# Folding both heads' softmax sums before the summing matmul, in the first four of eight batches

## The chip, the core and the metric

The kernel runs on one core of one Trainium2 chip. The metric is the time of one execution on the device in microseconds (us); lower is better. The core's engines are TensorE (PE, matmuls and transposes), VectorE (DVE), ScalarE (ACT), GpSimd (POOL) and SyncE (SP, which here only issues DMAs). Each engine takes its instructions in program order and waits on semaphores for the others.

## The reference

Blockwise causal attention, whose output feeds a mixture-of-experts layer with one expert for each token.

```python
# attention: batch 8, heads 8, sequence 576, head size 64, block 64
scores = scale * np.matmul(q, k.transpose(0, 1, 3, 2))
scores = np.where(mask, scores, -1e9)          # key block <= query block
attn = np.exp(scores - max); attn /= attn.sum(-1) + 1e-09
out = np.matmul(attn, v)                       # -> x: (8, 576, 512)

# experts: 8 of them, 512 -> 1024 -> 512
logits = x @ w_gate                            # (8, 576, 8)
local_gate = sigmoid(x @ w_local)
for b in range(B):
    for s in range(S):
        e = argmax(logits[b, s]) if s == 0 or local_gate[b, s] < 0.5 else prev_e
        out[b, s] = softmax(logits[b, s])[e] * (relu(x[b, s] @ w1[e]) @ w2[e])
```

## The kernel before, in words

**Attention.** The 64 heads are taken as 32 pairs, four pairs to a batch; the main loop runs over the pairs, `i = 0 .. 31`, with `b, r = divmod(i, 4)`. Order within each engine is the order of the program text. A pair's 576 keys are cut in five chunks (four of 128, one of 64) that lie on the partitions; the 576 queries lie along the free axis. So the exponentials of the scores stand as (keys, head, queries). Those of chunk 0 are written to `Ss[i]`, a 128 x 2 x 576 float32 tile from a ring of three (`Sall`), those of chunks 1 to 4 to `Pc[i % 2]`.

**One iteration** does, in this order: `load_qk(i + 2)` (SP's DMA queue); `values(i - 1)` (TensorE, L920, then a ScalarE copy to `oT`); `add_chunks(i - 1)` (VectorE, L932: four adds put chunks 1 to 4 onto `Ss[i - 1]`, in place, so they wait until `values` has read chunk 0); `load_v(i + 1)` (SP); `scores` and `exps` of pair `i` (TensorE L882, ScalarE L892, with GpSimd clearing the masked corners, L869, in `clear`); `transposes(i + 1)` of queries and keys (TensorE L844, ScalarE L839, and the VectorE copy L850 of the last 64 tokens); a task of the routing, if there is one; and `arrange(i + 2)`, two GpSimd copies (L810) that reorder the loaded queries and keys, followed in some iterations by a load of expert weights (L107, L111) on GpSimd's DMA queue. `load_qk` writes a staging buffer that `arrange` must have read first, so its DMA waits on SP for GpSimd, and what stands behind it on SP waits too. In iteration 1 alone `values(i - 1)` comes after the scores and `add_chunks(i - 1)` after the transposes (`swap`).

**The sums.** After `add_chunks`, row k of `Ss[i][:, h]` holds, for each query, the exponentials of the keys k, k + 128, ... of head h. The softmax's denominator is the sum of these over the 128 partitions. `half_batch(b, a)` (L696) takes it on TensorE together with the gate logits of two pairs, in one PSUM bank of four 32-row strips (two pairs, two ranges of 320 queries). It has three terms of four matmuls each: one that multiplies `oT` with the gate weights `wg2`, and two, one for each head, that multiply `Ss[i][:, h]` with a shifted view of `sel`, a tile that has a column of ones; the shift decides whether the sum lands in the head's row E + 1 or 16 + E + 1 of the strip. VectorE then copies the bank out (L704). The first half of a batch (pairs 0 and 1) is done at `r == 2`, the second half at `r == 0` of the next batch; each needs the sums of pair `i - 1`, whose adds run in the same iteration. At `r == 1` and `r == 3` the tasks are the logits' transposes and the rows of x (L718, L710, L757).

**Routing and experts.** From `slot >= 17.5` on VectorE also does the routing tables (`tokens`, `slots_first`), with scratch space in the last expert's part of `w1_bf`, which is loaded late for that reason. After pair 31 the expert stage runs over tiles of 128 gathered tokens (L994, L1128, gathers L653 and scatters L1135 on GpSimd).

Of the kernel before, what the change touches and what calls it, by code (L numbers as in the profile page):

```python
# [62 lines left out]
def kernel(  # L63
# [11 lines left out]
    nc = tc.nc  # L75
    F32 = mybir.dt.float32
# [5 lines left out]
    B, H, S, D = q.shape  # L82
# [4 lines left out]
    E = moe_w_gate.shape[1]  # L87
    F = moe_w1.shape[2]
    BS = B * S
    P = 128  # L90
# [11 lines left out]
    w1_bf = w_p.tile([P, E * KO1 * F], BF16, tag="w1", name="w1_bf")  # L102
    w2_bf = w_p.tile([P, E * FO * Dm], BF16, tag="w2", name="w2_bf")
    WE = KO1 * F
# [10 lines left out]
    HP = H // 2  # L115
# [31 lines left out]
    rt_c = ctx.enter_context(tc.tile_pool(name="rt_const", bufs=1))  # L147
# [3 lines left out]


    sel = rt_c.tile([P, 48], F32, tag="sel", name="sel")
    more_g = rt_c.tile([P, 256], F32, tag="more_g", name="more_g")

    wg2 = rt_c.tile([P, HP, 32], F32, tag="wg2", name="wg2")
# [519 lines left out]
    def bank(nm):  # L676
        return banks["of"](nm)
# [7 lines left out]
    def half_batch(b, a, gates=True, sums=True):  # L685


        ps = bank("trg")
        terms = [lambda i: (wg2[:, i % HP, :], oTs[i])] * gates + [
            lambda i, h=h: (sel[:, 16 - 16 * h:48 - 16 * h], Ss[i][:, h]) for h in range(2)] * sums  # L690
        for j, term in enumerate(terms):
            for p in range(2):
                w, x = term(HP * b + 2 * a + p)
                for g, q0 in enumerate((0, QA)):
                    o = 64 * g + 32 * p
                    nc.tensor.matmul(ps[o:o + 32, :QB], lhsT=w, rhs=x[:, q0:q0 + QB],  # L696
                                     start=(j == 0), stop=(j == len(terms) - 1))

        def out():
            if not gates:  # L700
                nc.vector.tensor_add(LT[b, a], LT[b, a], ps[:, :QB])
                return
            LT[b, a] = op.tile([P, QB], F32, tag="LT%d" % a, name="LT%d" % a, bufs=1)
            (nc.vector.tensor_copy if sums else nc.scalar.copy)(LT[b, a], ps[:, :QB])  # L704
        return out
# [41 lines left out]
    def rows_out(b, t):  # L747
        n = CW[t]
        ps = bank("trx")
        for p in range(HP):  # L750
            turn(ps, P * p, oTs[HP * b + p], t)

        def out():

            x = (xgs[t][:, :XH] if b < NB1 + 1 or (b < B - 1 and t == NX - 1)
                 else op.tile([P, XH], F32, tag="x", name="x"))
            nc.vector.tensor_mul(x[:n].bitcast(BF16).rearrange("p (h d) -> p h d", d=D),  # L757
                                 ps[:n].rearrange("p (h d) -> p h d", d=D),
                                 rcp(b, t)[:, :, None].to_broadcast([n, H, D]))
            r0 = b * S + P * t  # L760
            store(x_dram[r0:r0 + n, :XH], x[:n])
        return out

    oTs, rs, LT, Ss = ({} for _ in range(4))

    with tc.tile_pool(name="atn_const", bufs=1) as cst, \
# [13 lines left out]
        def constants():  # L780
            nc.vector.memset(sel, 0.0)
            nc.vector.memset(sel[:, 16 + E + 1:16 + E + 2], 1.0)
            nc.vector.memset(L[64:, :, :], 0.0)

        raws, vs = ({} for _ in range(2))
# [27 lines left out]
        def load_v(i):  # L813
            if i >= NPAIR:
                return
            b, p = divmod(i, HP)
            m = ld.tile([P, 4, 2, D], F32, tag="v4", name="v4", bufs=NV)
            for h in range(2):
                nc.sync.dma_start(
                    out=m[:, :, h, :],  # L820
                    in_=v[b, 2 * p + h, :512].rearrange("(so si) d -> si so d", si=P))
            nc.sync.dma_start(out=vls[i % NV][:ST],
                              in_=v[b, 2 * p:2 * p + 2, 512:].rearrange("h s d -> s h d"))
            vs[i] = [m, vls[i % NV]]
# [101 lines left out]
        def add_chunks(i):  # L926
            if not 0 <= i < NPAIR:
                return
            for c in range(1, NC):
                n = S - P * c  # L930
                rows = slice(0, CW[c])
                nc.vector.tensor_add(Ss[i][rows, :, P * c:], Ss[i][rows, :, P * c:],  # L932
                                     Pc[i % 2][rows, :, POS[c]:POS[c] + n])

        def tasks(i):

            b, r = divmod(i, HP)
            if r == 0 and b:
                return [[lambda: half_batch(b - 1, 1)]]
            if r == 1 and b:  # L940
                return [[lambda: logits(b - 1, 0), lambda: logits(b - 1, 1)],
                        [lambda t=t: rows_out(b - 1, t) for t in (0, 1)]]
            if r == 2:
                return [[lambda: half_batch(b, 0)]]
            if r == 3 and b:
                return [[lambda t=t: rows_out(b - 1, t) for t in (2, 3)],
                        [lambda: rows_out(b - 1, 4)]]
            return []
# [24 lines left out]
        sums = [Sb[(NPAIR + j) % NSB].rearrange("p h s -> p (h s)") for j in (1, 2, 0)]  # L973
# [28 lines left out]
        def expert(ph, j, engines=(mybir.EngineType.PE, mybir.EngineType.DVE)):  # L1002
            return nc.values_load(
                et_i[ph][0:1, j:j + 1], engines=engines, min_val=0,
                max_val=(E - 1) * WE,
                skip_runtime_bounds_check_because="the table is clamped to the last expert")

        def bf(x, n):
            return x.rearrange("p a s -> p (a s)").bitcast(BF16)[:, :n]
# [27 lines left out]
        def behind(i):  # L1037

            values(i - 1)
            if not swap:  # L1040
                add_chunks(i - 1)
            load_v(i + 1)
            steps.vector(1.4)

        for i in range(NPAIR):
            slot[0] = i
            load_qk(i + 2)


            swap = i == 1  # L1050
            if not swap:
                behind(i)
            if i == NPAIR - 1:

                tiles = [(0, j) for j in range(NS[0])] + [(1, j) for j in range(NS[1])]
                ev = {j: expert(*tiles[j]) for j in range(2)}
                w = weights_at(bf(Pc[0], WE), ev[0])

                free = bf(Sb[(NPAIR - 3) % NSB], 2 * S * 2)[:, -AHEAD * Dm:]
                xTs = {}  # L1060
                for j in range(AHEAD):
                    xTs[j] = free[:, j * Dm:(j + 1) * Dm].rearrange("p (k n) -> p k n", k=KO1)
                    nc.sync.dma_start(out=xTs[j], in_=row_of_x(xgs[j]), transpose=True)
            for u in range(len(UNITS)):
                exps(i, u, scores(i, u))
                if u == 0:
                    last_scores(i)
                    if i == 0:
                        transposes(1, nc.vector.tensor_copy)
                        constants()  # L1070
                        for h in range(2):
                            hs = slice(64 * h, 64 * h + 64)
                            nc.sync.dma_start(
                                out=wg2[hs, :, 16 * h:16 * h + E],
                                in_=moe_w_gate.rearrange("(p h d) e -> h d p e", h=2, d=D)[h])
                            nc.sync.dma_start(
                                out=wg2[hs, :, 16 * h + E:16 * h + E + 1],
                                in_=moe_w_local.rearrange("(p h d) e -> h d p e", h=2, d=D)[h])
            if swap:
                behind(i)  # L1080
            if i:
                transposes(i + 1, nc.scalar.copy)
            if swap:
                add_chunks(i - 1)
            for x in pending.pop(0) if pending else []:
                x()
            steps.tensor()
            steps.vector(2.0)
            for group in tasks(i):
                half.clear()  # L1090
                for out in [x() for x in group]:
                    out()
            slot[0] = i + 0.5
            if i == NPAIR - 1:

                w_next = weights_at(qkT.rearrange("p j a s -> p (j a s)").bitcast(BF16)[:, :WE],
                                    ev[1])
            steps.tensor()
            steps.vector(2.7)
            arrange(i + 2, [nc.gpsimd.tensor_copy] * 2)  # L1100

            if i == 1 + 25 * wload // 13 and wload < 2 * E - 2:
                load_weights(*divmod(wload, 2))
                wload += 1
            if i == NPAIR - 2:

                load_weights(E - 1, 1)
# [13 lines left out]
    with tc.tile_pool(name="ffn_s", bufs=2) as f_p, \  # L1121
# [148 lines left out]
        i = len(tiles) - 1  # L1270
# [31 lines left out]
```

## Time and profile before

| | us |
|---|---|
| three runs | 445.13, 449.56, 449.73 (median 449.56) |
| the profiled execution | 444.11 |
| its span, first to last instruction | 442.2 |
| TensorE busy (matmuls) | 423.8 (96% of the span) |
| VectorE busy | 255.1 (58%) |
| ScalarE busy | 257.6 (58%) |
| GpSimd busy | 185.3 (42%) |
| add_chunks, L932, 128 adds on VectorE | 90.3 |
| summing term, L696, 256 records trg<-S | 21.3 |
| arrange, L810, 61 copies on GpSimd | 44.2 |

A row of the profile names the line, the engine, the operation, the tile written and the tiles read, the shape and a count; `x` ahead of a number is that count. "idle before" is how long the engine stood still before the row's instructions, with what ended most of it behind an arrow. A busy TensorE is not one at its peak, since its matmuls overlap. The names `w1_bf` and `w2_bf` both appear as `w_bf`, and the staging buffer of queries and keys lies in `w2_bf`, so `w_bf<-in_k_dram` is a load of keys and `w_bf<-w_bf` a copy of `arrange`.

### The profile page before, as it was taken

Reading aid. Unit: us, or ns where it says so; the run is one execution under the profiler, and the core shown is the slowest. Engines: PE = TensorE matmul, PEld = TensorE weight load, DVE = VectorE, ACT = ScalarE, POOL = GpSimd, SP = SyncE. Lnnn points to the kernel's source line nnn. Section 1 sums busy time; section 2 is a strip of 40 time slices with the busy share of each in tenths; the row PEclk is TensorE's granted clock in tenths of the full one; section 3 lists DMA queues with packets and bytes.
Section 4 is the critical chain, followed back from the end, with each engine's and each line's share of the span. In section 5 each row is a group of like instructions: output and inputs, shape, how many; then the busy total and the mean of one; then the engine's idle time right before and its main releaser. Section 6 shows DMA issues by size and latency. Waiting matters only on the chain.

```text
span 442.2 us, 11716 instructions
## 1 busy us (share of the span) xinstructions
PE 423.8 (96%) x4260; PEld 309.3 (70%) x4281; DVE 255.1 (58%) x554; ACT 257.6 (58%) x409; POOL 185.3 (42%) x309
## 2 busy tenths in 40 slices
PE   8997999999999999999999999999799999999995
PEld 6775777677687676776776778657577767767763
DVE  3362454563563467868789976887788433333320
ACT  3763676577567656665677567534354545555552
POOL 2433423223212312123323514315757777767733
PEclk9997999999999999999999999999999999999999
DMA  5598399889799897986989884972847465556441
GB/s 161 138 209 167 92 199 190 187 185 181 182 180 185 181 190 174 191 125 145 183 171 215 156 217 75 188 130 87 167 133 159 114 159 137 147 142 151 134 104 72
DMA packets 113817, 69.65 MB, mean 157 GB/s; under 512 B 77024, under 2 KB 106208, under 8 KB 113761
## 3 DMA queue, kind: packets, MB, share of 16 engines
q1 hardware_dynamic: 96352, 37.94, 37.8%
q0 software_dynamic: 17408, 30.96, 34.9%
q8 instruction: 36, 0.59, 0.6%
q14 instruction: 21, 0.16, 0.1%
HBM read 66.88 MB, written 14.70 MB: 184 GB/s over the span
## 4 chain that ended last, share of the span: by engine, by line
PE 64%; DMA 14%; POOL 8%; issue 7%; ACT 4%; DVE 2%; POOLq 1%; SPq 1%; ACTq 0%; DVEq 0%
PE o L920 19%; PE sc L882 17%; PE trg L696 6%; PE kq L844 6%; DMA xg<-x_rows,idx 6%; PE ps_h L994 5%; POOL xg L653 5%; PE ps_y L1128 4%; DMA v<-in_v_dram 3%; PE trx L710 3%; POOL out_dram L1135 2%; DMA xT<-xg 2%; ACT Pc L892 2%; DMA w_bf<-in_q_dram 1%; DMA w_bf<-in_k_dram 1%
## 5 line engine op out<-in xcount | busy, mean ns | idle before, releaser
L932 DVE TENSOR_TENSOR S<-S,Pc 128x896 f32<-128x896 f32 (+3 forms) x128 | 90.3, 706 | 21.0 <-PE o L920 12.8
L882 PE MATMUL sc<-qkT 64*128 64x288 f32 (+3 forms) x768 | 98.8, 390 | 0.1
L882 PEld LDWEIGHTS sc<-qkT 64*128 64x128 f32 x768 | 68.8, 187 | 14.0 <-ACT qkT L839 0.5
L979 DVE COPY w1c<-w_bf 128x4096 bf16 x36 | 44.5, 1236 | 57.3 <-PE ps_h L994 53.7
L994 PEld LDWEIGHTS <-w1c 128*128 128x128 bf16 x1152 | 67.0, 98 | 13.0 <-issue 4.1
L994 PE MATMUL ps_h<-xT,w1c 128*128 128x128 bf16 x1088 | 66.3, 219 | 4.2 <-DMA xT<-xg 2.9
L924 ACT COPY oT<-o 128x576 f32<-128x576 f32 x32 | 20.5, 639 | 84.8 <-PE o L920 73.9
L1128 PE MATMUL ps_y<-w_bf,hT 128*128 x283 | 67.6, 379 | 1.1
L653 POOL DMA_INDIRECT xg<-x_rows,idx x38 | 56.1, 1477 | 23.1 <-issue 10.2
L839 ACT COPY qkT<-kq 128x1024 f32<-128x1024 f32 (+1 forms) x31 | 64.7, 2087 | 1.8 <-PE kq L844 1.6
L892 ACT ACTIVATE Pc<-sc 128x448 f32<-128x448 f32 (+1 forms) x96 | 63.9, 707 | 0.0
L810 POOL COPY w_bf<-w_bf 128x512 f32<-128x512 f32 x61 | 44.2, 745 | 44.1 <-DMA w_bf<-in_k_dram 20.0
L997 ACT ACTIVATE hT<-ps_h 128x512 bf16<-128x512 f32 x76 | 45.3, 597 | 29.4 <-PE ps_h L994 26.1
L920 PE MATMUL o<-Pc,v 128*64 128x320 f32 (+2 forms) x512 | 59.8, 373 | 0.0
L1135 POOL DMA_INDIRECT out_dram<-y,idx x38 | 44.1, 1160 | 35.3 <-ACT y L1133 20.2
L920 PEld LDWEIGHTS o<-Pc,v 128*64 128x64 f32 x512 | 36.9, 140 | 23.5 <-issue 0.2
L1133 ACT ACTIVATE y<-ps_y,xg 128x512 f32<-128x512 f32 x38 | 26.1, 688 | 45.1 <-PE ps_y L1128 43.2
L892 ACT ACTIVATE S<-sc 128x576 f32<-128x576 f32 x64 | 41.6, 650 | 15.6 <-PE sc L882 15.6
L1128 PEld LDWEIGHTS <-hT 128*128 128x128 bf16 x304 | 28.2, 98 | 27.7 <-issue 0.5
L869 POOL MEMSET Pc<- 64x128 f32 x96 | 17.5, 200 | 63.4 <-ACT Pc L892 59.4
L920 PE MATMUL o<-S,v 128*64 128x256 f32 (+1 forms) x256 | 39.7, 425 | 3.4 <-DMA v<-in_v_dram 2.5
L869 POOL MEMSET S<- 64x128 f32 x32 | 6.4, 200 | 86.5 <-ACT S L892 85.3
(287 smaller groups left out, 424.8 us busy)
## 6 DMA issues: line engine op xcount, KB each, us to landing
w_bf<-in_moe_w_dram POOLq DMA_DIRECT2D x16, 1024.0 KB, 10.4
w_bf<-in_k_dram SPq DMA_DIRECT2D x32, 256.0 KB, 3.6
w_bf<-in_q_dram SPq DMA_DIRECT2D x32, 256.0 KB, 4.5
v<-in_v_dram SPq DMA_DIRECT2D x64, 128.0 KB, 3.0
x_rows<-xg SPq DMA_DIRECT2D x24, 128.0 KB, 5.1
qkl<-in_k_dram SPq DMA_DIRECT2D x32, 32.0 KB, 3.7
qkl<-in_q_dram SPq DMA_DIRECT2D x32, 32.0 KB, 7.7
vl<-in_v_dram SPq DMA_DIRECT2D x32, 32.0 KB, 2.7
```

Source lines behind the costliest of these rows:

```text
L653: nc.gpsimd.indirect_dma_start(out=x, out_offset=None, in_=x_dram[:rows], in_offset=bass.IndirectOffsetOnAxis(ap=row_of(ph, j), axis=0), b ...
L810: copies[j](m, raws[i][1 + j].rearrange("p h j d -> p j h d"))
L839: copy(qkTs[i % 2][:, parts, :512].rearrange("p a (s j) -> p a j s", j=4), ps.rearrange("p a (j s) -> p a j s", j=4))
L882: nc.tensor.matmul(ps[:, h, col:col + n], lhsT=t[r, 0, c * P:c * P + P], rhs=t[r, 1, q0:q0 + n], start=True, stop=True)
L892: nc.scalar.activation(exps_at(i, c, q0, n, rows), ps[rows, :, col:col + n], func=AF.Exp, scale=scale_attn)
L920: nc.tensor.matmul(po[64 * h:64 * h + 64, VO + q0:VO + q0 + n], lhsT=vv, rhs=exps_at(i, c, q0, n, slice(0, P))[:, h, :], start=(c == 0), s ...
L932: nc.vector.tensor_add(Ss[i][rows, :, P * c:], Ss[i][rows, :, P * c:], Pc[i % 2][rows, :, POS[c]:POS[c] + n])
L979: nc.vector.tensor_copy(w, w1_bf[:, bass.ds(ev, WE)])
L994: nc.tensor.matmul(ps[:, fo, :], lhsT=w[:, ko * F + f0:ko * F + f0 + P], rhs=xT[:, ko, :], start=(ko == 0), stop=(ko == KO1 - 1))
L997: nc.scalar.activation(hT[:, half * (FO // 2):(half + 1) * (FO // 2), :], ps, func=AF.Relu)
L1128: nc.tensor.matmul(ps, lhsT=hT[:, fo, :], rhs=w2_bf[:, bass.ds(ev + fo * Dm, Dm)], start=(fo == 0), stop=(fo == FO - 1))
L1135: st = nc.gpsimd.indirect_dma_start(out=out_flat, out_offset=bass.IndirectOffsetOnAxis(ap=row_of(ph, j), axis=0), in_=y, in_offset=None, b ...
```

## The change

For pairs 0 to 15 the partitions' halves exchange their sums. `exchange(i)` has GpSimd copy the upper 64 partitions of head 0's sums to the lower 64 partitions of a buffer `swapped`, and the lower 64 of head 1's to the upper 64. `fold(i)` has VectorE add them, in place: afterwards the lower 64 partitions of `Ss[i][:, 0]` hold head 0's sums over 64 rows, and the upper 64 hold head 1's. One matmul term with `sel2`, a tile with a one in row E + 1 for the lower partitions and in row 16 + E + 1 for the upper, then gives both heads' denominators. `exchange` stands right behind `add_chunks` in the program, ahead of the iteration's clears and of `arrange` on GpSimd; `fold` stands behind the scores and ahead of the transposes, so ahead of L850 on VectorE (in iteration 1 both follow `add_chunks`). `swapped`, two buffers of 128 x 576 float32, lies at the end of the last expert's part of `w1_bf`. Batches 4 to 7 stay as they were.

```diff
+    sel2 = rt_c.tile([P, 32], F32, tag="sel2", name="sel2")
+
+    FOLDED = 4 * (H // 2)
...
         ps = bank("trg")
-        terms = [lambda i: (wg2[:, i % HP, :], oTs[i])] * gates + [
-            lambda i, h=h: (sel[:, 16 - 16 * h:48 - 16 * h], Ss[i][:, h]) for h in range(2)] * sums
+        terms = [lambda i: (wg2[:, i % HP, :], oTs[i])] * gates
+        if sums and HP * b < FOLDED:
+            terms += [lambda i: (sel2, Ss[i][:, 0])]
+        elif sums:
+            terms += [lambda i, h=h: (sel[:, 16 - 16 * h:48 - 16 * h], Ss[i][:, h])
+                      for h in range(2)]
...
             nc.vector.memset(sel[:, 16 + E + 1:16 + E + 2], 1.0)
+            nc.vector.memset(sel2, 0.0)
+            for h in range(2):
+                nc.vector.memset(sel2[64 * h:64 * h + 64, 16 * h + E + 1:16 * h + E + 2], 1.0)
...
+        swapped = w1_bf[:, E * WE - 4 * S:].bitcast(F32).rearrange("p (u s) -> p u s", u=2)
+
+        def exchange(i):
+            if 0 <= i < FOLDED:
+                for h in range(2):
+                    nc.gpsimd.tensor_copy(swapped[64 * h:64 * h + 64, i % 2],
+                                          Ss[i][64 - 64 * h:128 - 64 * h, h])
+
+        def fold(i):
+
+            if 0 <= i < FOLDED:
+                for h in range(2):
+                    r = slice(64 * h, 64 * h + 64)
+                    nc.vector.tensor_add(Ss[i][r, 0], Ss[i][r, h], swapped[r, i % 2])
...
             if not swap:
                 add_chunks(i - 1)
+                exchange(i - 1)
             load_v(i + 1)
...
             if swap:
                 behind(i)
+            else:
+                fold(i - 1)
             if i:
                 transposes(i + 1, nc.scalar.copy)
             if swap:
                 add_chunks(i - 1)
+                exchange(i - 1)
+                fold(i - 1)
```

## The prediction

> **What bounds the kernel now.** I read the page's busy table first, then the chain that ended last, then one stretch of time in the attention stage, then the groups of instructions kept apart by shape. The page says that TensorE is nearly always occupied and that most of the chain runs through it:
>
> ```profile
> PE 423.8 (96%) x4260; PEld 309.3 (70%) x4281; DVE 255.1 (58%) x554; ACT 257.6 (58%) x409; POOL 185.3 (42%) x309
> ...
> PE 64%; DMA 14%; POOL 8%; issue 7%; ACT 4%; DVE 2%; POOLq 1%; SPq 1%; ACTq 0%; DVEq 0%
> ```
>
> The chain between 120 and 140 us holds TensorE alone, so a microsecond taken from TensorE there is a microsecond of the kernel, and a microsecond that TensorE waits is one lost. Two pieces of it:
>
> ```profile
> 134.73 1.75 PE trg L696 x24
> 136.49 2.85 PE o L920 x28
> ```
>
> The first is one half_batch. In the timeline its gate term and its two sum terms stand apart, beside what GpSimd and VectorE do:
>
> ```profile
> 130.32 2.99 DVE L932 TENSOR_TENSOR S<-S,Pc 128x896 f32<-128x896 f32 x4
> ...
> 134.66 0.75 PE L696 MATMUL trg<-oT,wg 128*32 128x320 f32 x8
> 134.92 0.35 POOL L869 MEMSET Pc<- 64x128 f32 x2 [1.82 <-ACT Pc L892]
> 135.23 1.26 PE L696 MATMUL trg<-S,sel 128*32 128x320 f32 x16
> 135.34 1.18 POOL L810 COPY w_bf<-w_bf 128x512 f32<-128x512 f32 x2
> 136.41 0.20 PEld L920 LDWEIGHTS o<-S,v 128*64 128x64 f32 x4 [0.52 <-POOL w_bf L810]
> ```
>
> The gate term starts at 134.66, the sum terms at 135.23, the next work at 136.41. Two sum terms take 1.18 us, one takes 0.59. (A matmul shows as two records; 432 ns each is a latency, they overlap.) The adds of add_chunks end at 133.31, some 2.2 us before the first matmul that reads the newer pair's sums.
>
> **What is removed.** In eight half-batches (two for each of batches 0 to 3) four of twelve matmuls go: 8 x 0.59 = 4.7 us of TensorE. This is the ceiling of the gain, 1.05% of 449.6.
>
> **What is added, for each of 16 pairs.** Two GpSimd copies and two VectorE adds, each 64 x 576. The adds: the 896 form alone takes 1.09 us and the 384 form 0.56, so 1.04 ns for an element and 0.76 us for 576; two in a row overlap by 0.08, as the pair of L757 does (1.27 for 2 x 0.68), so 1.44. The copies: the nearest row is L810, 512 elements, 1.17 or 1.18 us for two; by length 1.31 for two of 576. No row shows a copy that moves data to other partitions. Its lower bound is that 1.31. For an upper bound I take twice that, 2.6, as near the 2.59 us that two L810 copies took when VectorE was in their way. I use 1.31, the same engine, type and kind, and keep 2.6 for the range. Three memsets of sel2 lie in iteration 0, where VectorE is idle for 6.39 us before L850: nothing, and 0.3 us if that cover were gone.
>
> **Copies and adds take turns.** One stretch shows what these two engines do to each other:
>
> ```profile
> 51.53 2.03 POOL L810 COPY w_bf<-w_bf 128x512 f32<-128x512 f32 x2
> 51.78 2.46 DVE L932 TENSOR_TENSOR S<-S,Pc 128x896 f32<-128x896 f32 x2 [0.71 <-PE o L920]
> ```
>
> The first copy took 0.61, the second 1.48: it ended only after the first add had. The two adds took 1.31 and 1.04 in place of 1.09 and 0.83. So a copy that is under way holds back an add, a copy that waits gets in between two adds, and each such copy costs VectorE some 0.22. In the new chain the second copy starts before the first fold add is released, so the order is copy, copy, add, add. With E the end of the adds: copies end at E + 1.31, the first fold add at about E + 1.95 (part of its fixed time is spent waiting), the second at E + 2.65. TensorE needs it for the second pair's matmul, the third of its sum term, 0.29 after the sum term starts.
>
> **Who is behind.** On VectorE the tail copy L850 stands behind the folds and ends up to 1.2 us later; its reader is scores of the next iteration, over 3 us on: hidden. On GpSimd the clears (L869), arrange (L810) and the weight DMA issue stand behind exchange; the clears had ended 1.5 us before values needs them at 136.41, and GpSimd was idle 4 to 5 us ahead of them, so in the steady part arrange starts where it did. On SP load_qk waits for arrange, load_v stands behind load_qk; this matters only at the start.
>
> **The sum, in three kinds of half-batch.** (1) Second halves, i = 4, 8, 12, 16: the adds end early (i = 8: 80.49; folds 83.14; needed 83.89; at i = 16 149.54, 152.19, 152.58), so the full 0.59 is gained: -2.4. (2) First halves, i = 6, 10, 14: VectorE is busy with the logits and rows of the batch before, adds end at 64.59, 99.22, 133.31; folds at 67.24, 102.09, 136.18 (in the last two an arrange copy comes in between, +0.22); needed at 66.82, 101.17, 135.52. With 0.1 for the signal TensorE waits 0.5, 1.0 and 0.8, 2.3 in all, against 3 x 0.59 = 1.8 saved: +0.5. Bounds: no wait, -1.8; each arrange copy ahead of a fold by its full 0.59, +1.6. (3) The first half-batch, i = 2, where two pairs' sums follow each other without a gap:
>
> ```profile
> 19.28 6.34 DVE L932 TENSOR_TENSOR S<-S,Pc 128x896 f32<-128x896 f32 x8
> ...
> 19.40 2.59 POOL L810 COPY w_bf<-w_bf 128x512 f32<-128x512 f32 x2 [2.69 <-DMA w_bf<-in_k_dram]
> 21.94 0.96 POOL L107 DMA_DIRECT2D w_bf<-in_moe_w_dram  x1
> ```
>
> Now: adds(0) end at 22.3, exchange(0) 23.6, arrange(3), which stood at 19.40, runs in among fold(0) and ends at 25.7 (before 21.99: +3.7); adds(1) 25.2 to 28.4, exchange(1) 29.7, fold(1) 31.2. TensorE would need it at 27.4 and idles some 3.9 us. What follows an idle time is shown two iterations on, where v comes late; the chain:
>
> ```profile
> 24.43 14.40 DMA v<-in_v_dram
> 38.88 5.59 PE o L920 x23
> ```
>
> The engines' busy times in stretches of 2 us around it say what that did to TensorE:
>
> ```profile
> 34.00:36.00 2.00, 1.57 (x13) 1.16 (x11) 0.29 (x1) 2.00 (x4) 0.35 (x2) 1.00 1.18 232
> 36.00:38.00 2.00, 0.34 (x2) 0.00 (x0) 0.00 (x0) 1.27 (x1) 0.00 (x0) 0.97 1.22 212
> 38.00:40.00 2.00, 1.12 (x5) 0.85 (x7) 0.00 (x0) 0.00 (x0) 0.00 (x0) 0.50 0.99 189
> 40.00:42.00 2.00, 2.00 (x12) 1.73 (x11) 0.80 (x1) 0.00 (x0) 1.08 (x2) 0.50 0.22 51
> 42.00:44.00 2.00, 2.00 (x12) 1.62 (x9) 1.79 (x3) 0.00 (x0) 1.80 (x6) 0.50 0.44 144
> ```
>
> (Last three columns: granted clock, share of the DMA engines, GB/s.) After 2.5 us without v the clock was 0.50 until about 44.6, and values took 5.59 in place of 2.85: 2.7 lost besides the wait. A wait of 1.9 us at 316 left the clock at 1.00. So 3.9 us at i = 2 most likely halves the clock too. Then TensorE resumes at 31.3, has 8.4 us of work up to values(3) (27.33 to 35.72 before), loses 2.7 to the clock and is there at 42.4. Load_v(3) waits on SP behind arrange(3) and shifts by 3.7: v lands at 42.5 in place of 38.84. The old wait is thus used up by the new one: values(3) runs 42.5 to 45.4 at full clock, where it ended at 44.47. Taken with half a microsecond of doubt on the landing: +1.5, with -1 to +6 as bounds. On the price of the slow clock the Trainium skill differs (TensorE: Matmul & The Clock Gate, Part 1: The HAM clock gate): about 3.4 us of steady work bring the full clock back. This trace shows 5.7 us from 38.88 to 44.6; by the page's figure the slow stretch would cost 1.7, an estimate, and the whole sum would stand near 1 us lower.
>
> Sum: -2.4 + 0.5 + 1.5 = -0.4 us. The profiled execution took 444.11 (span 442.2 and 1.9 around it), so 443.7 there. The runs shown are 445.13, 449.56 and 449.73, the median 5.5 above the profiled one; the kernel spreads over 1% by itself. On the median: 449.2.
>
> **The rivals.** *All of it is hidden* (444.9): copies and adds overlap, the fold is ready at every sum term and the start moves nothing: 449.6 - 4.7. For it: second halves have slack of 0.4 to 0.8. Against it: the 1.48 us copy, and i = 2, where GpSimd and VectorE have a chain of some 9 us where there was 6.3. Chance 0.12.
>
> *The copy to other partitions is dear* (457.7, the slower side): 1.31 us more for each exchange. Place: GpSimd, between adds and folds. First halves +3.9; second halves at i = 8, 12, 16 have slacks of 0.76, 0.76 and 0.44, so +2.0; at the start two exchanges, +2.6. That is 8.5 above the forecast. It decides for slower from about 0.8 us more for an exchange (2.4 + 1.2 + 1.6). For it: no row shows such a copy, GpSimd's times vary most. Against it: L810 has the same element count per partition and rearranges in runs of 64 at no visible cost. Chance 0.20.
>
> *The stall at the start doubles* (453.8): the clock halves at i = 2 and v still lands late, near 45, so that TensorE idles and slows again: values(3) ends at 45 + 5.6 = 50.6, 6.1 after 44.47, where I counted 1.5. For it: the DMA engines are at a share of 1.2 then. Against it: the weight loads that crowd v shift with it. Chance 0.15.
>
> *The term is not removed where it says*: the program's order shows four matmuls with S where there were eight, up to i = 16. No chance kept.
>
> **How the numbers follow.** Forecast 0.53, rivals 0.12, 0.20, 0.15. Faster or slower counts from 1%, about what a measurement of this kernel can tell from no change. Faster: the first rival, 0.12. Slower: the dear copy and two thirds of the doubled stall, which lies at the edge, 0.30. The rest, 0.58, is within. The range goes from full hiding, 445, to the dear copy, 458; the forecast's own is 446.5 to 452.5.
>
> **What would show it.** After: 8 records of trg<-S in a half-batch; copies near 0.65 us, back to back, fold adds only after the second; TensorE idle 0.5 to 1 us before trg at i = 6, 10, 14, none at 8, 12, 16; some 4 us idle and a clock of 0.50 near 30, and no wait for v near 40. Copies over 1 us with VectorE idle, or two slow-clock stretches, would prove me wrong upward; a fold that ends ahead of its sum term at i = 2, downward.

## The result, and the profile after

The kernel after takes 451.13 us (median of 22 runs, 445.76 to 457.20) beside 445.22 for the kernel before on the same chip (22 runs, 442.64 to 452.61). The ratio is 1.0104 with a 95% interval of 1.0081 to 1.0126: the change costs about one per cent. The ratio compares the fast runs alone, those within 1.5% of the fastest run of their kernel, and so it is smaller than that of the medians; the profiled execution after is not one of them. It took 452.61, its span 450.8. In this profile add_chunks is L943, arrange L821, values L931, half_batch L704, scores L893, the clears L880; the exchange copies are L952 and the fold adds L960.

The page's busy table and the shares of the chain that ended last:

```profile
PE 422.0 (94%) x4196; PEld 306.4 (68%) x4217; DVE 279.3 (62%) x589; ACT 254.5 (56%) x409; POOL 207.0 (46%) x341
...
PE 53%; issue 13%; DMA 10%; DVE 9%; POOL 9%; ACT 4%; POOLq 1%; SPq 0%; DVEq 0%; ACTq 0%
```

TensorE has 64 records fewer and is busy 1.8 us less, VectorE has 24 us more and GpSimd 22. VectorE stood for 2% of the chain before and stands for 9% now: TensorE waits for it somewhere. The chain itself, in the same two stretches as before (start, length, what):

```profile
29.25 13.64 DMA v<-in_v_dram
...
42.94 4.58 PE o L931 x23
...
120.03 1.22 PE trg L704 x16
121.25 2.85 PE o L931 x28
```

In the steady part the half-batch is what was wanted: 1.22 us with 16 records, where it was 1.75 with 24. At the start, v lands at 42.89 where it landed at 38.84, and values runs slowly behind it. The timeline shows the first half-batch (i = 2, the first eight lines) and the third (i = 6):

```profile
24.09 2.61 POOL L821 COPY w_bf<-w_bf 128x512 f32<-128x512 f32 x2
26.76 0.66 PE L855 MATMUL kq<-id_f,w_bf 128*128 128x128 f32 x4 [0.76 <-POOL w_bf L821]
28.02 0.71 PE L704 MATMUL trg<-S,sel 128*32 128x320 f32 x4
28.11 2.02 POOL L952 COPY w_bf<-S 64x576 f32<-64x576 f32 x2 [0.50 <-DVE S L943]
28.86 0.75 DVE L960 TENSOR_TENSOR S<-S,w_bf 64x576 f32<-64x576 f32 x1 [0.56 <-POOL w_bf L952]
30.17 0.76 DVE L960 TENSOR_TENSOR S<-S,w_bf 64x576 f32<-64x576 f32 x1 [0.56 <-POOL w_bf L952]
30.98 0.73 PE L704 MATMUL trg<-S,sel 128*32 128x320 f32 x4 [2.25 <-DVE S L960]
31.64 1.19 PE L931 MATMUL o<-S,v 128*64 128x256 f32 x8
...
66.84 2.03 POOL L952 COPY w_bf<-S 64x576 f32<-64x576 f32 x2 [5.13 <-DVE S L943]
67.59 0.75 DVE L960 TENSOR_TENSOR S<-S,w_bf 64x576 f32<-64x576 f32 x1 [0.56 <-POOL w_bf L952]
68.34 0.74 PE L704 MATMUL trg<-oT,wg 128*32 128x320 f32 x8
68.90 1.55 PE L704 MATMUL trg<-S,sel 128*32 128x320 f32 x8
68.90 0.76 DVE L960 TENSOR_TENSOR S<-S,w_bf 64x576 f32<-64x576 f32 x1 [0.56 <-POOL w_bf L952]
```

At i = 2 the first pair's sum term starts at 28.02 and the second pair's only at 30.98: 2.96 us from one to the other, where it is 0.3 without a wait. TensorE also waited for arrange, which now runs behind the first exchange: 0.76 here, and 0.32 a little earlier. At i = 6 the two copies and two adds alternate (copy, add, copy, add), and the sum term takes 1.55 instead of 0.72.

Busy times in stretches of 2 us at the start (stretch, its length, then TensorE's matmuls, TensorE's weight loads, VectorE, ScalarE and GpSimd with counts; the three last columns are the granted clock, the share of the DMA engines, GB/s):

```profile
28.00:30.00 2.00, 0.72 (x8) 0.12 (x2) 1.03 (x2) 1.57 (x1) 1.83 (x2) 1.00 1.04 200
30.00:32.00 2.00, 1.02 (x8) 0.43 (x10) 1.29 (x3) 0.00 (x0) 1.94 (x8) 1.00 1.05 187
32.00:34.00 2.00, 2.00 (x22) 1.17 (x20) 1.27 (x2) 0.00 (x0) 0.84 (x1) 1.00 1.12 202
...
40.00:42.00 2.00, 0.26 (x2) 0.00 (x0) 0.00 (x0) 0.75 (x1) 0.00 (x0) 1.00 1.18 235
42.00:44.00 2.00, 1.06 (x5) 0.79 (x7) 0.00 (x0) 0.00 (x0) 0.00 (x0) 0.73 1.19 221
44.00:46.00 2.00, 2.00 (x13) 1.73 (x11) 0.75 (x1) 0.00 (x0) 1.18 (x2) 0.50 0.30 69
```

The new wait, at 28 to 31, left the clock at 1.00. The old wait for v is there again, and it does halve the clock. Its two pieces, in the timeline of before (first two lines) and of after:

```profile
35.72 0.62 PE L920 MATMUL o<-S,v 128*64 128x256 f32 x2 [0.43 <-POOL Pc L869]
38.88 1.65 PE L920 MATMUL o<-S,v 128*64 128x256 f32 x5 [2.54 <-DMA v<-in_v_dram]
...
39.65 0.62 PE L931 MATMUL o<-S,v 128*64 128x256 f32 x2 [0.93 <-DMA v<-in_v_dram]
42.94 1.65 PE L931 MATMUL o<-S,v 128*64 128x256 f32 x5 [2.67 <-DMA v<-in_v_dram]
```

In after TensorE is ready at 38.7 and waits 3.6 us in all; in before it is 3.0, the first 0.43 of it for a clear.

**Iteration by iteration.** The start of scores (first L893, before L882) in the timeline marks each iteration. Distances from scores(i) to scores(i + 1) in us, each from one profiled execution; the kernels named e1 to e12 come below:

| i | before | e11 (before again) | after | e5 (after again) | e7 (start only) | e9 (reordered) | e2 (side work) | e8 (first halves) | e12 (all but first) |
|---|---|---|---|---|---|---|---|---|---|
| 2 | 8.75 | 8.75 | 12.25 | 13.94 | 12.25 | 13.45 | 11.97 | 8.75 | 8.76 |
| 3 | 13.33 | 7.50 | 12.96 | 7.51 | 7.50 | 7.50 | 9.32 | 7.50 | 7.50 |
| 4 | 8.90 | 8.76 | 8.21 | 8.21 | 8.76 | 8.21 | 8.93 | 8.76 | 8.21 |
| 6 | 8.76 | 8.75 | 9.04 | 9.54 | 8.75 | 9.65 | 9.25 | 8.99 | 9.56 |
| 8 | 8.75 | 8.75 | 8.21 | 8.21 | 8.75 | 8.22 | 8.75 | 8.76 | 8.21 |
| 10 | 8.75 | 8.76 | 9.21 | 9.21 | 8.76 | 8.98 | 8.91 | 8.97 | 9.21 |
| 14 | 8.75 | 8.75 | 8.99 | 9.41 | 8.75 | 9.00 | 8.75 | 8.98 | 9.23 |
| 16 | 8.75 | 8.76 | 8.21 | 8.22 | 8.76 | 8.22 | 8.75 | 8.76 | 8.22 |
| 4 to 16, all | 111.93 | 111.80 | 110.62 | 111.75 | 111.80 | 111.16 | 112.84 | 112.50 | 111.94 |

Three things stand out. The iterations with a second half-batch (4, 8, 16, and 12 likewise) are 0.54 us shorter. Those with a first one (6, 10, 14) are longer. And i = 2 is 3.5 us longer. The 13.33 at i = 3, on which much of the prediction rests, is not there in every execution of the kernel before.

The profiled pair differs by 8.6 us of span: 3.05 have been lost by scores(4) (47.45 against 44.40), 1.3 are won back by scores(17), 0.4 lost up to scores(31), and 6.5 lie behind it, in the expert stage (167.0 us from scores(31) to the end, against 160.5). That last part can't be put down to the change: e5, the same kernel, took 159.9 there.

### The profile page after: what moved, and what is told of

It is laid out like the page before. It is cut to its first block, busy times and chain, and to the rows that moved or that the text cites. A ratio compares the mean times of both kernels' runs of the same rounds, so it can differ in the third digit from the quotient of the medians.

```text
span 450.8 us, 11654 instructions
## 1 busy us (share of the span) xinstructions
PE 422.0 (94%) x4196; PEld 306.4 (68%) x4217; DVE 279.3 (62%) x589; ACT 254.5 (56%) x409; POOL 207.0 (46%) x341
## 2 busy tenths in 40 slices
DMA packets 113817, 69.66 MB, mean 155 GB/s; under 512 B 77023, under 2 KB 106207, under 8 KB 113760
## 4 chain that ended last, share of the span: by engine, by line
PE 53%; issue 13%; DMA 10%; DVE 9%; POOL 9%; ACT 4%; POOLq 1%; SPq 0%; DVEq 0%; ACTq 0%
PE o L931 16%; PE sc L893 14%; DMA xg<-x_rows,idx 5%; PE ps_h L1021 5%; PE kq L855 5%; PE trg L704 5%; PE ps_y L1160 4%; POOL xg L657 4%; DVE S L943 4%; DMA v<-in_v_dram 3%; PE trx L718 2%; POOL out_dram L1167 2%; POOL w_bf L952 2%; ACT Pc L903 2%; DMA w_bf<-in_q_dram 1%
## 5 line engine op out<-in xcount | busy, mean ns | idle before, releaser
L943 DVE TENSOR_TENSOR S<-S,Pc 128x896 f32<-128x896 f32 (+3 forms) x128 | 89.8, 702 | 21.1 <-PE o L931 12.7
L893 PE MATMUL sc<-qkT 64*128 64x288 f32 (+3 forms) x768 | 98.7, 389 | 0.7 <-ACT qkT L850 0.6
L893 PEld LDWEIGHTS sc<-qkT 64*128 64x128 f32 x768 | 68.7, 187 | 14.5 <-ACT qkT L850 0.9
L1021 PE MATMUL ps_h<-xT,w1c 128*128 128x128 bf16 x1088 | 67.8, 219 | 9.0 <-ACT hT L1024 5.6
L1167 POOL DMA_INDIRECT out_dram<-y,idx x38 | 51.2, 1348 | 50.3 <-ACT y L1165 32.5
L850 ACT COPY qkT<-kq 128x1024 f32<-128x1024 f32 (+1 forms) x31 | 64.2, 2071 | 2.3 <-PE kq L855 2.2
L931 PE MATMUL o<-Pc,v 128*64 128x320 f32 (+2 forms) x512 | 58.9, 370 | 0.0
L821 POOL COPY w_bf<-w_bf 128x512 f32<-128x512 f32 x61 | 42.8, 725 | 25.6 <-DMA w_bf<-in_k_dram 10.4
L952 POOL COPY w_bf<-S 64x576 f32<-64x576 f32 x32 | 31.6, 986 | 47.9 <-DVE S L943 46.9
L931 PEld LDWEIGHTS o<-Pc,v 128*64 128x64 f32 x512 | 36.6, 139 | 23.4 <-issue 0.2
L657 POOL DMA_INDIRECT xg<-x_rows,idx x38 | 42.1, 1107 | 21.3 <-issue 11.8
L931 PE MATMUL o<-S,v 128*64 128x256 f32 (+1 forms) x256 | 39.7, 425 | 4.5 <-DMA v<-in_v_dram 3.6
L855 PE MATMUL kq<-id_f,w_bf 128*128 128x128 f32 x256 | 36.1, 283 | 1.4 <-POOL w_bf L821 1.0
```

Source lines behind the costliest of these rows:

```text
L657: nc.gpsimd.indirect_dma_start(out=x, out_offset=None, in_=x_dram[:rows], in_offset=bass.IndirectOffsetOnAxis(ap=row_of(ph, j), axis=0), b ...
L850: copy(qkTs[i % 2][:, parts, :512].rearrange("p a (s j) -> p a j s", j=4), ps.rearrange("p a (j s) -> p a j s", j=4))
L855: nc.tensor.transpose(ps[:, j * P:j * P + P], raws[i][1 + part][:, j].rearrange("s h d -> s (h d)"), id_f)
L893: nc.tensor.matmul(ps[:, h, col:col + n], lhsT=t[r, 0, c * P:c * P + P], rhs=t[r, 1, q0:q0 + n], start=True, stop=True)
L931: nc.tensor.matmul(po[64 * h:64 * h + 64, VO + q0:VO + q0 + n], lhsT=vv, rhs=exps_at(i, c, q0, n, slice(0, P))[:, h, :], start=(c == 0), s ...
L1021: nc.tensor.matmul(ps[:, fo, :], lhsT=w[:, ko * F + f0:ko * F + f0 + P], rhs=xT[:, ko, :], start=(ko == 0), stop=(ko == KO1 - 1))
```

## The experiments

They ran on three chips (e1 to e4, e5 to e8, e9 to e12), each time beside runs of the kernel before (medians 439.28 to 439.46 there, against 445.22 in the first comparison); ratios are to those, and a gain or loss in us is worked out from the ratio. The expectations weigh three readings of the loss, named in the first of them: the start, a slower rhythm of the expert stage, and contention of the copies and adds.

**e1 and e2: the change cut in two.** e1 removes the term and adds nothing, so that head 1 gets head 0's denominators, which are wrong for it; e2 adds everything and removes nothing.

```diff
# e1_term_only: head 0's sums with ones for both heads
-                nc.vector.memset(sel2[64 * h:64 * h + 64, 16 * h + E + 1:16 * h + E + 2], 1.0)
+                nc.vector.memset(sel2[:, 16 * h + E + 1:16 * h + E + 2], 1.0)
...
-            if 0 <= i < FOLDED:          # in exchange and in fold
+            if 0 <= i < 0:
# e2_side_work
-        if sums and HP * b < FOLDED:
+        if sums and HP * b < 0:
...
-                    nc.vector.tensor_add(Ss[i][r, 0], Ss[i][r, h], swapped[r, i % 2])
+                    nc.vector.tensor_add(swapped[r, i % 2], Ss[i][r, h], swapped[r, i % 2])
```

> Only the removal: batches 0 to 3 have one sum term instead of two, with nothing exchanged or folded (the term reads head 0's sums for both heads, so head 1's denominators are head 0's). Theory start (the stall at i = 2 and the late v behind it are the loss, the expert stage is only chance): nothing stalls, TensorE gains 8 x 0.57 = 4.6 us up to i = 17, the whole time goes down by 4 to 5 us, ratio near 0.990. Theory rhythm (the expert stage falls into a slower rhythm, 3.9 us a tile in place of 3.5, when anything moves the engines against each other): 4.6 gained by i = 17 and 3 to 7 given back after 345 us, ratio 0.995 to 1.005. Theory contention (the copies and adds are the loss): as theory start, 0.990.

> Only the additions: exchange and fold run for pairs 0 to 15 but the fold writes into the swapped buffer, and both sum terms stay, so TensorE does what it did and waits for no fold. Theory start: arrange(3) still comes some 3 us later, v(3) with it, values(3) ends 2 to 3 us later than 44.4 and the rest follows; ratio 1.004 to 1.007, steady iterations unchanged at 17.3 us for two. Theory contention: two iterations take 0.3 us or more longer as well, ratio 1.010 or more. Theory rhythm: an expert stage at 3.9 us a tile in its second part whatever the start does, ratio 1.01.

e1: 434.92, ratio 0.991 (0.9874 to 0.9947), 4.0 us gained. e2: 443.73, ratio 1.0117 (1.0071 to 1.0164), 5.1 us lost. So the removal is worth nearly what the prediction's ceiling says (8 x 0.59 = 4.7): in e1's profile scores(4) to scores(17) take 108.03 instead of 111.80, seven times 0.54. The additions cost as much or more without any reader of the fold. Where e2 pays is in its timeline:

```profile
26.90 0.66 PE L855 MATMUL kq<-id_f,w_bf 128*128 128x128 f32 x4 [0.76 <-POOL w_bf L821]
...
30.23 0.20 POOL L880 MEMSET S<- 64x128 f32 x1
30.37 0.49 POOL L880 MEMSET Pc<- 64x128 f32 x3
...
31.49 1.19 PE L931 MATMUL o<-S,v 128*64 128x256 f32 x8 [1.74 <-POOL Pc L880]
```

TensorE waits 0.76 for arrange as after does, and 1.74 at values: the clears stand behind the second exchange on GpSimd and end at 30.9. So two chains end at about 31 in iteration 2: the fold, and the clears behind the copies. Taking one away leaves the other.

**e3 and e4: where in the four batches.** e3 folds from batch 1 on, e4 only in the second half-batches.

```diff
# e3_later_start
-        if sums and HP * b < FOLDED:
+        if sums and HP <= HP * b < FOLDED:
...
-            if 0 <= i < FOLDED:
+            if HP <= i < FOLDED:
# e4_second_halves
-        if sums and HP * b < FOLDED:
+        if sums and a and HP * b < FOLDED:
...
-            if 0 <= i < FOLDED:
+            if 0 <= i < FOLDED and i % HP >= 2:
```

> Exchange, fold and the single term from batch 1 on (pairs 4 to 15), batch 0 as before. Theory start: values(3) ends at 44.4 as before, then -0.55 at i = 8, 12, 16 and +0.3 at i = 6, 10, 14, so 0.6 us faster or no change, ratio 0.997 to 1.000. Theory rhythm: the same gain up to the expert stage, then 3 us or more given back, ratio near 1.007. Theory contention: ratio 1.005 or more with the loss spread over i = 6 to 17.

> Exchange, fold and the single term only for the second half of batches 0 to 3 (pairs 2, 3, 6, 7, 10, 11, 14, 15; half-batches at i = 4, 8, 12, 16), where the fold was ready in time. Theory start: the first half-batch stands as it was, four times -0.57, so 2.3 us faster, ratio 0.995. Theory rhythm: the same up to i = 17, then lost again in the expert stage, ratio 1.000 to 1.005. Theory contention: half of the copies and adds, ratio above 1.003.

e3: 437.22, ratio 0.9975 (0.9943 to 1.0008). e4: 435.69, ratio 0.9945 (0.9917 to 0.9974). Without batch 0 the loss is gone, and the second halves alone are a version that beats the kernel before, by 2.4 us: four terms of 0.54 are 2.2.

**e5 to e8: the same kernels again, and the other parts alone.** e5 is the kernel after and e6 the kernel before, unchanged. e7 folds pairs 0 and 1 alone, e8 the first half-batches of batches 1 to 3.

```diff
# e7_start_only
-        if sums and HP * b < FOLDED:
+        if sums and b == 0 and a == 0:
...
-            if 0 <= i < FOLDED:
+            if 0 <= i < 2:
# e8_first_halves
-        if sums and HP * b < FOLDED:
+        if sums and a == 0 and HP <= HP * b < FOLDED:
...
-            if 0 <= i < FOLDED:
+            if HP <= i < FOLDED and i % HP < 2:
```

> The changed kernel as it is, once more. Theory start: TensorE waits some 3 us in iteration 2 and v(3) comes some 3 us later than in the kernel before; by i = 5 it stands 3 to 5 us behind, gets back 4 x 0.55 at i = 4, 8, 12, 16 and loses 3 x 0.33 at i = 6, 10, 14; ratio 1.005 to 1.010, with the expert stage at 3.5 us a tile in a run that is not disturbed. Theory rhythm: the expert stage stands at 3.9 us a tile from the fifteenth tile on in this profile too, ratio 1.010 to 1.015.

> The kernel before, unchanged, for a profile on the same chip as its neighbours. Ratio 1.000. Theory start expects it to reach the half-batch at i = 2 at 26.5 us and values(3) near 35.7 without a wait on GpSimd; whether v(3) is late there tells whether the 5 us lost in the first profile belong to that chip. Theory rhythm expects the expert stage at 3.5 us a tile.

> Exchange, fold and the single term for pairs 0 and 1 alone, so only the half-batch at i = 2. Theory start: this alone costs 3 to 5 us, ratio 1.007 to 1.012, and the rest of the attention stage keeps the old pace of 17.3 us for two iterations. Theory rhythm: 1.000 to 1.005 unless the expert stage falls into the slower pace.

> Exchange, fold and the single term for pairs 4, 5, 8, 9, 12 and 13, so the half-batches at i = 6, 10 and 14. Theory start with the steady waits as measured (0.83, 1.0 and 0.78 us of waiting against 0.57 saved): +0.9 us, ratio 1.002. Theory contention: 1.005 or more. Theory rhythm: 1.002 or 1.010, by the pace of the expert stage.

e5: 443.07, ratio 1.0071 (1.0031 to 1.0112). e6: 438.68, ratio 0.9991 (0.995 to 1.0031). e7: 442.74, ratio 1.0079 (1.0043 to 1.0115). e8: 438.45, ratio 0.9982 (0.9945 to 1.002). The first half-batch, one of eight, costs 3.5 us by itself and so accounts for the whole loss on this chip. That bears out the reading by the start. Contention would have had e8 at 1.005 or more, and the slower rhythm would have lengthened the expert stage, which takes 159.1 us in e7 and 159.9 in e5, against 167.0 in after. e7 and e5 have the same code up to there and the same wait; what the clock does behind it differs. e7, timeline:

```profile
30.84 0.73 PE L704 MATMUL trg<-S,sel 128*32 128x320 f32 x4 [2.25 <-DVE S L960]
...
32.52 1.79 PE L931 MATMUL o<-Pc,v 128*64 128x128 f32 x16
```

e5, timeline:

```profile
30.77 0.73 PE L704 MATMUL trg<-S,sel 128*32 128x320 f32 x4 [2.25 <-DVE S L960]
...
32.68 3.25 PE L931 MATMUL o<-Pc,v 128*64 128x128 f32 x16
```

And e5 in stretches of 2 us, with the granted clock third from the right:

```profile
30.00:32.00 2.00, 1.23 (x10) 0.57 (x12) 1.46 (x3) 0.00 (x0) 1.94 (x7) 1.00 1.11 202
32.00:34.00 2.00, 2.00 (x14) 1.18 (x12) 1.00 (x2) 0.00 (x0) 0.63 (x1) 0.55 1.15 207
34.00:36.00 2.00, 2.00 (x16) 1.08 (x12) 1.76 (x4) 0.00 (x0) 0.14 (x1) 0.60 1.17 272
```

Sixteen matmuls take 1.79 us in the one and 3.25 in the other. Iteration 2 is 13.94 instead of 12.25: the halved clock costs 1.7 where it comes.

**e9 to e11: can the start be reordered, and is it the code or the memory.** In e9 the whole change is kept, but exchange(i - 1) of the early iterations is issued behind arrange and the weight load on GpSimd, and fold(0) beside fold(1) in iteration 2. e10 has sel2 and its memsets but no fold. e11 is the kernel before, one profiled execution.

```diff
# e9_reordered, in the loop body
+                if i == 2:
+                    fold(0)
...
-                exchange(i - 1)
-                fold(i - 1)
...
+            if swap:
+                exchange(i - 1)
# e10_control
-    FOLDED = 4 * (H // 2)
+    FOLDED = 0 * (H // 2)
```

> The whole change, but at the start exchange(0) stands behind arrange(3) and the weight load on GpSimd, and fold(0) beside fold(1) in iteration 2. Theory start (GpSimd's and VectorE's queues at i = 1 and 2 are the cost): arrange(3) runs at 19.4 us again, no wait before the transposes, v(3) no later than in the kernel before; the sum term at i = 2 waits 1 to 1.5 us in place of 2.7; with the steady -1.2 the ratio is 0.996 to 1.001, against 1.007 for the change as it is. Theory rhythm or contention: 1.006 or more, as before the reordering.

> The tile sel2 and its three memsets stay, but nothing is exchanged or folded and all sum terms are the old ones. Theory start, with the late v(3) of the kernel before a matter of chance: ratio 1.000 within 0.003. If the place of the tiles in memory or the three memsets decide whether v(3) is late: 0.990 to 0.995, and v in time in the profile.

> The kernel before once more, for a profile: whether v(3) is late again (values(3) starts near 39 in place of 35.8). Theory start takes the late v as chance and gives no side; if the place in memory decides, it is late again.

e9: 442.34, ratio 1.0063 (1.0034 to 1.0093): not recovered, against what the theory expected. e10: 438.91, ratio 0.9993 (0.996 to 1.0026): the tile and its memsets cost nothing. e11: 437.72. The timeline of e9 tells why the order didn't help:

```profile
19.19 7.09 DVE L943 TENSOR_TENSOR S<-S,Pc 128x896 f32<-128x896 f32 x8
...
26.20 4.21 DVE L960 TENSOR_TENSOR S<-S,w_bf 64x576 f32<-64x576 f32 x4
...
28.61 0.73 PE L704 MATMUL trg<-S,sel 128*32 128x320 f32 x4 [1.49 <-DVE S L960]
...
30.47 0.73 PE L704 MATMUL trg<-S,sel 128*32 128x320 f32 x4 [1.14 <-DVE S L960]
```

The wait for arrange is gone, and the DMA engines no longer pause: in after their share is 0.00 from 22 to 26 us, in e9 0.77 and 1.12. But VectorE has eight adds and four folds to do without a gap, from 19.19 to 30.41, and TensorE is ready at about 27. The start is bound by VectorE's and GpSimd's work for two pairs at once: in this order VectorE ends its folds at 30.41, in that of after at 30.93. Whether a third order would do better was not tried. Here the clock halved too (0.50 at 32 to 34), for 13.45.

**e12: all but the first half-batch.** The three parts by themselves, e7, e8 and e4, multiply to 1.0006, below e5's 1.0071. Either that is the spread, or the parts cost more together.

```diff
-        if sums and HP * b < FOLDED:
+        if sums and b + a > 0 and HP * b < FOLDED:
...
-            if 0 <= i < FOLDED:
+            if 2 <= i < FOLDED:
```

> The whole change except its first half-batch: pairs 0 and 1 are neither exchanged nor folded, their half-batch keeps both sum terms; the seven other half-batches of the four batches are as in the changed kernel. Theory start: the whole change cost 0.7% in the same-chip comparison and the start alone 0.8%, so without the start the rest is a small gain: a ratio of 0.994 to 0.998, start of iteration 3 8.75 us after that of iteration 2, no wait of TensorE for a fold there, and waits of some 0.3 to 0.9 us net left at iterations 6, 10 and 14. Rival interaction: the parts together cost more than each by itself (start alone 1.0079, first halves 0.9982 and second halves 0.9945 multiply to 1.0006, against 1.0071 for the whole), because exchanges, folds and weight copies of neighbouring pairs queue behind one another when all of them are there; then this kernel stays at 0.999 or above, and its iterations 6, 10 and 14 are longer than those of the kernel with the first halves alone (8.99, 8.97, 8.98).

e12: 439.70, ratio 1.0013 (0.9979 to 1.0048), so the rival's side, though the interval reaches down to the 0.998 of theory start: the seven other half-batches together gain nothing that the runs show, though the four second ones alone gain 0.55%. Its first halves are longer than in e8, by 0.57, 0.24 and 0.25 at i = 6, 10 and 14 (the table), and i = 5 takes 9.09 where it takes 8.53 in e8; at i = 6, from its timeline:

```profile
58.95 2.04 POOL L952 COPY w_bf<-S 64x576 f32<-64x576 f32 x2 [3.29 <-DVE S L943]
...
60.50 0.71 PE L704 MATMUL trg<-S,sel 128*32 128x320 f32 x4
61.02 0.75 DVE L960 TENSOR_TENSOR S<-S,w_bf 64x576 f32<-64x576 f32 x1 [0.56 <-POOL w_bf L952]
61.83 0.73 PE L704 MATMUL trg<-S,sel 128*32 128x320 f32 x4 [0.62 <-DVE S L960]
```

The second pair's term waits for the second fold add. That TensorE meets this wait because the second halves have become shorter, while VectorE's work has not, is a reading of the table and was not tested apart. Two profiles speak against it as the whole cause. In e9, which has the second halves too, i = 10 and 14 take 8.98 and 9.00, as in e8. And e4, which folds nothing at i = 6, took 9.75 there, because loads of queries came late:

```profile
55.17 1.13 POOL L821 COPY w_bf<-w_bf 128x512 f32<-128x512 f32 x1 [3.26 <-DMA w_bf<-in_q_dram]
...
59.86 0.30 PE L859 MATMUL o<-id_f,qkl 128*128 128x128 f32 x1 [0.80 <-DMA qkl<-in_q_dram]
```

The same copy of arrange waited 2.06 us for its load in e12 and 2.37 in e5, so part of their i = 5 and 6 may be due to a late load; this stays open. Products agree within the intervals: e7 times e12 is 1.0092, e7 times e3 (which leaves i = 4 as it was) 1.0054, around e5's 1.0071 and the first comparison's 1.0104.

## Why the prediction was wrong

It forecast no change (449.2, the sum -0.4 us), with slower by over 1% at 0.30; the change is slower by 1.0%. The range of 445 to 458 holds the time. By its steps:

- **What bounds the kernel, and the ceiling**: right. e1 gains 4.0 us where 4.7 was the ceiling; a term removed is worth 0.54 in an iteration, not 0.59, which makes 4.3.
- **Exchange and fold**: the order was predicted as copy, copy, add, add, and it is copy, add, copy, add. The pair of copies takes 2.03 us, not 1.31, since the second ends only after the first add has (68.87 against 68.34). The fold still ends 2.63 us after the adds (at i = 6: 69.66 against 67.03), and 2.65 was predicted; as the order was another, the agreement is in part luck. A copy with nothing beside it takes 0.72 us (e4), so the copy to other partitions is not dear, and the rival built on it falls. The Trainium skill describes such taking of turns (SBUF — State Buffer, "SBUF: two separate sides"): a VectorE instruction with two inputs in SBUF, as these adds are, and a GpSimd instruction that reads SBUF take a shared port pair for the whole instruction, and the other waits. The trace agrees: the second copy took 1.3 us beside an add of 0.75 and ended 0.5 after it.
- **Step (1), the second halves, -2.4**: right. No wait, four times 0.54, that is -2.2 in after.
- **Step (2), the first halves, +0.5**: too small. After has +0.29, +0.46 and +0.24, in all +1.0, e5 +1.9, e12 +1.75. The wait at i = 6 was put at 0.5 and is 0.83 in after; the two others, put at 1.0 and 0.8, are of that size. With (1) that leaves -1.2 in after and nothing in e5 and e12 (the last row of the table, beside e11's 111.80), where -1.9 was predicted.
- **Step (3), the start, +1.5: this step failed.** Its stall was predicted well: TensorE was to idle some 3.9 us. Beside e1, which has the removal alone, the sum term starts 1.1 us later after scores(2) (the wait for arrange) and values 3.0 later after the sum term (3.62 against 0.65): 4.0 together, and less the 0.5 of the removed term it is the 3.5 of iteration 2. What failed is "The old wait is thus used up by the new one". It rests on two readings. One is that the late v of the profiled execution belongs to the kernel. It doesn't: of four profiles of the kernel before or its equal (before, e6, e10, e11) two have it (e6's i = 3 is 13.02) and two don't, and of the five others that don't have the stall (e1, e3, e4, e8, e12) none. Where v is in time, i = 3 takes 7.50 and there is nothing to use up, and the stall counts in full: +3.5 in e7, +5.2 in e5, +4.7 in e9. The other is that the clock would halve at i = 2 and bring TensorE to v's landing. It landed nearly as predicted (42.89; 42.5 was said), but the clock held, TensorE was there at 38.7, waited 3.6 us and slowed down behind it. So in after, where v was late, the new wait came on top of the old. That is one profile; in e2 v was late by less, with i = 3 at 9.32 and the clock at 1.00.
- **The rivals**: the stall that doubles (453.8) is what the profiled execution after shows in part: both waits, but the slow clock at the second only, so that scores(4) starts 3.05 us later than before, where this rival has values(3) end 6.1 later. In e5, e7 and e9 the cause is simpler: one stall, paid in full. Full hiding is excluded by i = 2, 6, 10 and 14.
- **The median**: 449.56, from three runs, was itself high: 22 runs give 445.22, and five of them lie between 448.5 and 452.7. The profiled 444.11, which is not one of the 22, lies below that median although it has the late v, which speaks against the late v alone making the high runs.

With +3.5 for step (3), and -1.2 to 0 for (1) and (2), the sum is +2.3 to +3.5, and 1.7 more where the clock halves (2.7 was predicted for that); measured are 4.6 (1.04% of 445) and 3.1 (0.71% of 439).

**What stays open.** In the profile of after the expert stage runs in a slower rhythm from about 347 us on: two tiles from 370.39 to 378.21, 7.82 us, where e5 takes 7.03. Every second activation waits long for TensorE:

```profile
370.39 0.60 ACT L1024 ACTIVATE hT<-ps_h 128x512 bf16<-128x512 f32 x1 [0.27 <-PE ps_h L1021]
...
373.79 0.60 ACT L1024 ACTIVATE hT<-ps_h 128x512 bf16<-128x512 f32 x1 [2.80 <-PE ps_h L1021]
...
378.21 0.60 ACT L1024 ACTIVATE hT<-ps_h 128x512 bf16<-128x512 f32 x1 [0.26 <-PE ps_h L1021]
```

In the other profiles the expert stage takes 158.5 to 162.6 us, so it is no effect of the change that could be shown; whether more of its runs have it, and so part of the difference between 1.0104 and 1.0071, isn't known. Nor is it known why v comes late in some executions.

## What to carry to other kernels

A wait that a profile shows once, above all one for a DMA, may be that execution's alone: count it as cover for new work only after several profiles have shown it, and price the new stall without it as well. Work moved to idle engines is free only where these have slack at that place: 16 exchanges and folds of the same size were hidden at four half-batches, cost a little at three and 3.5 us at one, so look for the iteration in which the side engines have two pairs' work back to back. Leaving the change out of the expensive places (e4) turned a loss of 0.7% (e5) into a gain of 0.55%, each against the kernel before on its own chip.

## What the runs showed of the hardware

The same idle time need not do the same to the clock. In e7, after and e5 TensorE stood 2.25 us at the same place; the granted clock stayed at 1.00 in two and fell to 0.50 in the third, for 3.4 us beginning 1.4 us after work had resumed. In e9 two waits of 1.49 and 1.14 us were enough. The Trainium skill has a rule that would allow this (TensorE: Matmul & The Clock Gate, Part 1: The HAM clock gate): activity is watched in a free-running window of about 3.4 us, and when the clock changes depends on where in the window work begins. The traces agree in the length of the slow stretch, 3.4 us in e5, and differ from the Trainium skill, which has the clock drop after an idle window, where a gap shorter than a window was enough; that the window's phase decides is not shown here. Worked out from the granted clock in stretches of 0.5 us, the slow stretch is 3.4 us in e5, e6, e9 and after, and 6.8, twice that, in before; the prediction's 5.7 is the part of it in which TensorE had work.

A load of the same 128 KB, issued at the same place of the program, can land in time or leave TensorE waiting in two pieces, 0.43 (for a clear) and 2.54 us in before, 0.93 and 2.7 in e6 and after alike, and with the slow clock behind it costs 5.5 to 5.8 us: 13.33, 13.02 and 12.96 against 7.50 at i = 3.
